# A new order of operations for a fused Nyström attention and MLP kernel on one core

## The chip, the core and the metric

The kernel runs on one core of a Trainium2 chip. A core has a matrix engine (PE, with its weight loads shown as PEld), three engines for elementwise work (DVE, ACT and POOL), and SyncE (SP), which here only issues DMAs. Each engine has its own queue of instructions and works through it in program order; engines wait for one another through semaphores. The metric is the device time of one execution, in microseconds (us), as the median of several runs.

## What is computed

Eight batches of eight heads, 576 rows and 64 columns a head, first through a Nyström attention with 32 landmarks, then through an MLP with a layer norm before and the input added behind. Cut to what matters:

```python
q_lm = q.reshape(B, H, 32, 18, 64).mean(axis=3)
k_lm = k.reshape(B, H, 32, 18, 64).mean(axis=3)
A, Bm, C = sm(q, k_lm), sm(q_lm, k_lm), sm(q_lm, k)      # softmax of the scaled products
Z = Bm.T / (norm1(Bm) * norm_inf(Bm) + 1e-06)
for _ in range(6):
    Z = 2 * Z - Z @ Bm @ Z
attn = A @ Z @ C @ v
x = attn.transpose(0, 2, 1, 3).reshape(B, S, 512)
xn = (x - mean(x)) / sqrt(var(x) + 1e-06) * g_ln
out = x + relu(xn @ w_ch1) @ w_ch2                       # 512 -> 2048 -> 512
```

## The kernel before

**Tiling.** Batch 0 is worked by itself, then batch 1, then the sets of batches 2-3, 4-5 and 6-7 (the text calls these sets 2, 3 and 4, and batch 1 is a set of its own). For each set the attention part makes landmarks (lm, or tot and lmt in batch 1), the landmark products (psb, then the Gram matrix and six steps of the iteration), the weights C (psec, whose exponentials are ec, turned into ecT), their product with v (pscv), the last two small products (pszt and pszc, giving zt and zcbd) and the weights A (psea, whose exponentials ea are normalized through psd, lns and a multiplication). The iteration is a chain between two engines: PE's *step* writes `it`, DVE or ACT forms the *next* `st` from it, and the next step reads that.

The MLP follows by batch: psy gives x, which DVE measures (BATCH_NORM_STATS2, BATCH_NORM_AGGREGATE); psm, corrected by the less terms, gives m, the landmark part already multiplied by w1; psh = ea times m gives the hidden rows in two halves of 288, which ACT or DVE passes through a relu into hT; pso sums hT against w2 in sixteen pieces, and one DVE operation (the *done* of the block) adds x and writes the output rows, which a DMA stores. Four row blocks of batches 2 to 7 use a scheme of seven products instead (ps7a, ps7c, ps7e, with the sums mix on POOL and DVE). The last row block, 7-4, is done in two column parts, pso_74a (384 wide) and pso_74b (128 wide), and comes last.

**Small tiles.** pso, psh, psy, psd and the seven products use the whole 128 x 128 array. psm uses tiles of 64 x 32; psec, psea, the steps of sets 2 to 4, the Gram products and zc and zt use 32 x 32; pscv uses 64 x 64. On PE a run of such matmuls between whole-array ones is called a block of small tiles.

**Weights.** w1 comes in eight loads (load_w1_0 to load_w1_7, stg slots) on SP's queue, each followed by two scalings by g, scale_w1 at L357, on any of three engines. The less-mean matmuls (psf) read the scaled parts. Two slots of v, six of stg, two PSUM slots of kind p2 (for psh and psec among others) and four PSUM banks are the shared buffers of most interest (L296 to L305).

**What sets the order.** Every operation is defined once by a name, the engines that it may run on, and the buffers it uses. A list, ORDER (L19), names 1571 operations by number, each with a letter for its engine (P, D, A, G for POOL, S for SP). The operations are emitted in exactly this order:

```python
order = [(names[int(x[:-1])], x[-1]) for x in ORDER.split()]
for n, e in order:
    emit(n, e)
```

So the list decides each engine's program order, which engine does an operation that several can do, and which buffer of a pool it gets: `emit` (L174) takes the slot that was given back first, and gives a buffer back when its last user has been emitted. An operation that reuses a slot waits for the last user of its former content. Operations on DVE, ACT and POOL, and the DMA issues that stand in their queues, wait for the operation ahead of them even where their own inputs are ready.

At the start, `warm` (L309) puts idle matmuls (idle<-zeros) on PE at several places of the list.

Of the kernel before, what the change touches and what calls it, by code (L numbers as in the profile page):

```python
# [19 lines left out]
0G 20P 23P 4S 12P 14P 24P 17P 11P 2S 1S 3S 6S 7S 10P 21P 28G 38P 25A 26D 34P 39D 40P 29P 30A 31P 27D  # L20
37P 32P 42D 41D 18P 33D 43P 65P 44A 45D 66A 61P 67P 46P 47P 250G 48D 22P 19P 15P 62A 68A 69A 71D
245G 49P 50D 63P 35P 13P 79G 80D 51P 52D 64A 36A 81P 70D 53P 72P 73A 5S 95S 54D 8P 9D 105A 106G 55P
56D 57P 74P 82D 260P 83D 58D 16P 84D 96S 59P 75A 76A 60D 85P 251D 86D 89P 90D 87P 88D 126P 261A 262D
108G 77G 94S 103G 93S 97S 101G 91D 92D 78D 107A 102G 127P 128P 129P 130A 167P 141P 142A 252P 253A
145P 169D 104A 168D 98S 254D 149P 150D 147P 148A 172P 173A 176P 247P 177A 248A 259D 255D 174P 175A
246D 256P 257A 146A 170P 171D 109G 110G 121P 122P 123P 111G 124P 268P 156P 258D 151D 249D 267P 112A
125A 275A 269A 270A 271A 157D 277A 158D 131P 132P 133P 134P 178P 163P 278D 279D 117G 273A 433G 274A
99S 113G 135A 180D 263S 164A 159P 280P 281D 160A 165P 166A 114G 264A 100S 115G 116G 265S 118G 136P
137P 266G 161P 179D 429G 119G 138P 139P 162D 282P 283D 140A 181P 182A 183P 284P 276D 285A 143P 187P
184D 286P 144A 188A 272D 152D 185P 186A 287D 297P 298D 299D 189P 191D 190D 288P 289A 294P 290P 295A  # L30
201P 202P 296A 300P 301A 291D 292P 293A 120G 455G 212P 213P 435G 436G 437G 310P 438G 445G 302A 303G
308P 309A 214P 330P 434D 444D 312D 311D 313D 332D 192P 193A 153D 154D 198P 199A 155A 441D 430D 439D
431D 331D 442D 440D 432D 443D 234P 556D 215P 304P 235P 236P 305A 306A 196P 446G 447G 203P 204P 194P
195A 237P 238P 205P 206P 451G 197A 307G 314P 315A 337P 339P 448G 449D 822G 338A 555D 239P 240P 241P
322P 207P 208P 574D 565D 569G 450D 340A 323A 216P 242D 209D 210S 217P 324D 341P 343D 223P 335P 244S
336A 342D 333P 463D 218P 219P 577G 452D 220D 344P 352P 353D 467G 468G 469G 470G 334A 826G 348P 345A
349A 346P 347A 457G 318P 319A 224P 316P 317A 225P 226P 227P 481P 458G 465D 459G 460G 482A 350P 454D
354D 357P 471D 464D 472D 351A 453D 363P 228P 229P 364D 358A 361P 230P 362A 461D 462D 365D 493P 494A
359P 368P 360A 483P 495P 355P 325D 326D 505A 369A 356A 231D 233A 200G 374P 375P 366P 367A 370P 371A
573G 506D 456D 507P 508P 509D 320P 321D 385P 484P 486A 487A 489A 510P 834D 511D 466D 491A 386P 387P  # L40
485A 388P 211S 512P 376P 473S 474G 490A 377P 496P 498A 501A 499A 497A 513D 514P 327D 488D 492D 328D
396P 397P 475S 476G 566G 828G 829G 830G 831G 572G 477S 478G 838G 839G 844G 564G 568G 503A 378P 379P
380P 515D 823D 502A 221S 504D 372P 516P 479S 480A 500D 517D 836D 528P 529P 530D 531D 398P 399P 373A
381P 522P 518P 389P 329A 866S 382D 418P 519D 824D 559D 520P 521D 523A 532P 419P 420P 524A 533A 534A
558D 550P 551D 552D 553D 548P 549A 421P 422P 423P 536P 424P 425P 848G 535G 832D 833D 554D 232S 867A
537A 538A 539G 560D 525P 527A 400P 401P 557D 426D 427S 605P 526A 606A 840G 841G 594P 595A 561D 540P
541A 390P 391P 611P 612A 837D 596D 827D 392P 393D 825D 850G 851G 852G 563D 603P 604A 853G 562D 859D
842D 860G 861G 843D 579P 613P 614A 407P 580A 601P 602A 609P 610A 1217G 585P 408P 845D 599P 409P 607P
600A 410P 411P 586A 597P 608A 542A 543G 856D 615P 598A 576G 626P 616A 412P 413P 581P 627A 402P 862G
394S 582A 570G 567D 617D 589D 835D 863G 858D 590D 618P 619A 634P 635A 643P 583P 584A 620P 621A 624P  # L50
414P 571G 874P 625A 622P 623A 628P 629A 644P 544P 847D 857D 545A 846D 591D 546A 875D 403P 632P 872S
633A 645P 630P 647P 592D 631A 646P 415D 877P 648P 649P 650P 864D 865D 854D 404D 855D 1191G 886P 638D
637G 641G 663P 664P 665P 639D 640D 662G 428S 417S 406S 661D 593A 882A 884A 879A 880A 883A 652D 878A
651D 657D 887A 889P 892A 896A 658D 666P 668D 894A 895A 849D 667D 653P 654P 711P 722P 712A 723A 891A
890A 655P 656P 547G 575G 675P 676P 677P 728P 729A 678P 695P 696A 1192D 713D 716P 881D 1194D 717A
724P 725A 876P 888P 1213G 660D 587P 870S 714P 416S 659D 871G 873G 384S 1229G 642G 1230G 1231G 726P
898A 715A 679D 682D 669P 897D 727A 588A 730P 222S 1232G 899D 900P 901P 731A 718P 732P 902D 743P 719D
578G 903P 904D 670P 720P 734A 733A 721D 744A 671P 672P 673D 699P 700A 893D 739P 636G 1203D 1239S
701P 905P 243S 741P 906D 740A 751P 674D 742A 703P 752A 907P 735P 736A 737P 383S 868S 681S 680S 683S
738A 702D 908D 909P 1219G 1195G 1220G 1221G 685P 704D 697P 698A 915P 917A 916A 910D 911P 1222G 759P  # L60
760P 749P 811P 925P 750A 761P 885D 869G 921P 926A 927A 753G 922P 1225D 755G 912D 913P 705D 706D 745P
746A 1227D 812P 707D 708D 709D 710A 813P 814P 747P 748A 686P 687P 688P 928G 929P 930A 1223D 1224D
1196D 1233D 815P 816P 923D 1228D 924D 914D 931A 1214D 943P 947D 944D 941P 817P 946D 945D 1240G 754G
756G 932G 758G 942A 762P 692D 767D 694S 689D 818P 763P 764P 918P 765P 766P 395S 1241S 1197G 920A
1198G 1199G 1200G 919A 819D 963P 974P 965A 975A 1207G 1208G 1209G 768D 769P 964D 774D 770P 956P 968P
1215D 1204D 957A 966P 690S 693S 405S 773D 969A 1226D 779P 967A 933P 934A 935A 780P 972P 948P 949A
1234D 1216D 970P 781P 973A 936G 984P 985A 820S 771P 971D 757D 986D 980P 772P 978P 782P 954P 776D
1242A 775D 981A 979A 976P 977A 955A 937P 1193D 938A 939A 1205D 785P 786P 787P 788P 982P 983A 1255P
989P 990A 1210G 684S 783D 1211D 1212D 1201D 1202D 1243P 777G 778G 784D 790D 691S 991P 1244A 789D
992A 801P 1235S 995P 996A 1245P 940G 1236G 1256D 1257P 802P 1267A 1268D 987P 988A 803P 993P 994A  # L70
1066P 1067D 804P 808D 1269P 1270P 1237S 1238G 1246P 1249A 805D 791P 792P 810S 1206D 1271D 821S 1248A
1247A 1253A 1250D 1251A 793P 958D 794P 1006G 1252A 809S 1003P 1004A 1272P 798D 1273D 997P 998A 950P
951A 1001P 1218D 795D 1012P 999P 1002A 1000A 1007G 1009G 1274P 1008D 1275D 952P 953A 1072P 1258P
1073A 1265A 1264A 1276P 1013P 1014P 1015P 1263A 1261A 1260A 1064P 959D 960D 1016P 1259A 961D 962A
1017P 1284P 1285A 1065A 1277D 1278P 1018P 1019P 797S 800S 799S 1294P 1295A 1296A 1021D 1262D 1020D
1026D 1027D 1254D 1279D 1266D 1011G 1022P 1297G 1070P 1023P 1024P 1025P 1029D 1028D 1005G 1068P
1069D 1286A 1298P 1290P 1299A 1291P 1292D 1010D 1293D 1280P 1281D 1091P 1032P 1033P 1038P 1300A
1301G 1092A 1287P 1071D 1289A 1288A 1282P 1283D 1039P 1040P 1312P 1314D 1313D 1316D 1315D 1080P
1082A 796S 1099P 1100A 1081A 1034P 1035P 806S 1310P 1311A 1097P 1036D 1098A 1041P 1306P 1101P 1307A
1095P 1096A 1037D 1030D 1044P 1043D 1093P 1094A 1089P 1090A 1042D 1074D 1075D 1031G 807S 1045P 1046P  # L80
1083P 1084D 1047P 1103A 1051D 1317P 1318A 1087P 1088A 1102D 1085P 1086A 1054P 1052S 1055P 1106P
1107A 1104P 1048D 1049S 1105D 1319P 1320A 1056P 1057P 1061D 1076D 1108P 1058D 1109A 1110P 1111A
# [1181 lines left out]
```

## Time and profile before

| | us |
|---|---|
| median of 3 runs | 259.85 |
| lowest and highest | 259.77 and 260.1 |
| the profiled execution | 260.21 |
| its span in the profile | 258.5 |
| last matmul of block 7-4 ends | 254.6 |

The profiled execution is one more run, 0.36 us above the median. Its span, counted from the first instruction to the last, leaves 1.7 us around it. In the views of the profile a line such as L193 is that of the helper which records every matmul, so rows are told apart by tile names: `pso<-w,hT` writes the tile pso from w and hT. "x4" at a row's end is a run of like instructions, shown as one row with the time from the first one's start to the last one's end. A bracket tells how long the engine had been idle before the row, and what released it. Matmuls are pipelined, so the duration of one overlaps the next; distances between starts tell more.

### The profile page before, as it was taken

To read this page: it belongs to the slowest core of one execution; us is meant where nothing else is said; L and a number is where in the kernel's file an instruction comes from. 1 tells how busy PE (TensorE), PEld (TensorE's weight loads), DVE (VectorE), ACT (ScalarE), POOL (GpSimd) and SP (SyncE) were. 2 spreads that over 40 slices of the span, in tenths; PEclk is the share of its full clock that TensorE was granted. 3 is DMA by queue.
4 is the path that set the end of the run, shared out by engine and by line. 5 is a ranking of instruction groups with operands and counts; after the bars stand their busy time and mean duration, and the time that the engine had idled before them with its cause. 6 is when DMAs were issued, how large, how long until landed. Compare 5 with 4: busy or idle time off the path is not lost.

```text
span 258.5 us, 8352 instructions
## 1 busy us (share of the span) xinstructions
PE 249.3 (96%) x3499; PEld 178.4 (69%) x3499; DVE 212.1 (82%) x472; ACT 164.0 (63%) x304; POOL 177.6 (69%) x180
## 2 busy tenths in 40 slices
PE   7689999999999999999999999999999999999994
PEld 7566565555654457777776787777867787788882
DVE  1669899999999989996998879887537999878761
ACT  1588886737766899778756996878766246544000
POOL 8324899689893789699999996782068505966600
PEclk9999999999999999999999999999999999999998
DMA  6999999999749275949814832400130100500356
GB/s 236 364 281 341 365 207 202 207 230 258 230 121 161 44 160 80 207 100 279 144 21 111 235 96 63 114 16 3 41 85 0 44 20 3 122 22 14 90 120 185
DMA packets 23278, 36.32 MB, mean 140 GB/s; under 512 B 2117, under 2 KB 11593, under 8 KB 23241
## 3 DMA queue, kind: packets, MB, share of 16 engines
q1 hardware_dynamic: 12376, 23.34, 29.9%
q0 software_dynamic: 9504, 10.36, 25.3%
q10 hardware_dynamic: 1360, 2.10, 3.2%
q8 instruction: 27, 0.44, 0.7%
q14 instruction: 11, 0.08, 0.1%
HBM read 36.70 MB, written 9.44 MB: 178 GB/s over the span
## 4 chain that ended last, share of the span: by engine, by line
PE 88%; DMA 6%; ACT 2%; DVE 1%; issue 0%; POOL 0%; ACTq 0%; POOLq 0%
PE psh L193 24%; PE ps7a L193 16%; PE pso L193 15%; PE ps7c L193 8%; DMA nat_q<-in_q_dram 5%; PE ps7e L193 4%; PE psm L193 4%; PE psy L193 3%; PE it L193 3%; PE psec L193 2%; PE pscv L193 2%; DMA stg_k<-in_k_dram 2%; PE psd L193 1%; PE psea L193 1%; PE psf L193 1%; PE pso_74a L193 1%
## 5 line engine op out<-in xcount | busy, mean ns | idle before, releaser
L203 ACT ACTIVATE hT<-psh 128x576 f16<-128x576 f32 x106 | 65.8, 650 | 30.4 <-PE psh L193 28.6
L193 PEld LDWEIGHTS <-hT 128*128 128x128 f16 x688 | 64.4, 98 | 23.3 <-issue 3.7
L193 PE MATMUL psh<-ea,m 128*128 128x288 f16 x512 | 78.3, 287 | 0.1
L193 PEld LDWEIGHTS <-m 128*128 128x128 f16 x512 | 48.8, 98 | 15.7 <-issue 1.3
L193 PE MATMUL pso<-w,hT 128*128 128x512 f16 x176 | 45.7, 380 | 0.1
L207 POOL TENSOR_TENSOR mix<-hT 128x1024 f16<-128x1024 f16 x8 | 17.0, 2128 | 27.4 <-ACT hT L203 27.4
L210 DVE SCALAR_TENSOR_TENSOR x<-ps7a,rstd,x 128x256 f32<-128x256 f32 x48 | 21.3, 476 | 6.2 <-PE ps7a L193 4.4
L193 PE MATMUL ps7a<-mix,hT 128*128 128x256 f16 x192 | 25.6, 273 | 0.0
L1068 DVE TENSOR_SCALAR hT<-psh 128x576 f16<-128x576 f32 x22 | 16.4, 753 | 10.1 <-PE psh L193 9.9
L997 DVE BATCH_NORM_STATS2 six<-x 128x6 f32<-128x512 f32 x36 | 24.2, 673 | 0.0
L207 POOL TENSOR_TENSOR ea<-ea,lns 128x576 f16<-128x576 f16 (+1 forms) x14 | 17.7, 1261 | 8.0 <-ACT lns L203 4.3
L200 ACT CAST m<-psm 128x512 f16<-128x512 f32 (+1 forms) x25 | 19.1, 792 | 4.5 <-PE psm L193 3.4
L200 ACT COPY x<-psy 128x512 f32<-128x512 f32 (+1 forms) x29 | 16.8, 587 | 7.7 <-PE psy L193 7.3
L193 PEld LDWEIGHTS <-mix 128*128 128x128 f16 x192 | 18.3, 98 | 4.3 <-issue 1.5
L207 POOL TENSOR_TENSOR mix<-mix,hT 128x1024 f16<-128x1024 f16 x8 | 17.0, 2127 | 6.2 <-DVE mix L207 5.8
L207 POOL TENSOR_TENSOR hT<-hT 128x1024 f16<-128x1024 f16 x9 | 19.1, 2123 | 0.2
L207 POOL TENSOR_TENSOR hT<-hT,mix 128x1024 f16<-128x1024 f16 x7 | 15.1, 2169 | 4.4 <-PE ps7e L193 2.5
L214 DVE TENSOR_REDUCE part<-xT_k 128x32 f16<-128x576 f16 x24 | 17.1, 736 | 0.0
L207 POOL TENSOR_TENSOR asum_q<-asum_q 128x256 f32<-128x256 f32 (+1 forms) x24 | 15.1, 629 | 1.5
L203 ACT ACTIVATE ec<-psec 128x256 f16<-128x256 f32 (+1 forms) x42 | 12.4, 431 | 5.3 <-PE psec L193 5.3
L193 PE MATMUL psy<-zcbd,ea 128*128 128x256 f16 x80 | 14.8, 273 | 0.2 <-ACT x L200 0.2
L357 POOL TENSOR_SCALAR w<-w1s,g_sb 128x512 f16<-128x512 f32 x12 | 8.2, 693 | 9.4 <-DMA w1s<-in_moe_w_ch_dram 5.5
(174 smaller groups left out, 473.1 us busy)
## 6 DMA issues: line engine op xcount, KB each, us to landing
out_dram<-x SPq DMA_DIRECT2D x55, 128.0 KB, 2.6
stg_v<-in_v_dram SPq DMA_DIRECT2D x10, 576.0 KB, 5.9
w1s<-in_moe_w_ch_dram SPq DMA_DIRECT2D x8, 512.0 KB, 11.6
nat_q<-in_q_dram POOLq DMA_DIRECT2D x7, 576.0 KB, 8.3
nat_k<-in_k_dram POOLq DMA_DIRECT2D x7, 576.0 KB, 8.2
w<-in_moe_w_ch_dram POOLq DMA_DIRECT2D x4, 512.0 KB, 9.0
out_dram<-x ACTq DMA_DIRECT2D x15, 128.0 KB, 2.4
stg_v<-in_v_dram SPq DMA_DIRECT2D x6, 288.0 KB, 4.3
```

The costliest lines, as they stand in the source:

```text
L193: keep(nc.tensor.matmul(o, l, r, start=start, stop=stop, tile_position=(rb, cb), skip_group_check=(skip or cb != 0)))
L200: keep(nc.scalar.copy(o, i) if e == "A" else ENGINES[e].tensor_copy(out=o, in_=i))
L203: keep(nc.scalar.activation(*args, **kw))
L207: keep(ENGINES[e].tensor_tensor(out=o, in0=a, in1=b, op=f))
L210: keep(ENGINES[e].scalar_tensor_tensor(out=o, in0=a, scalar=s, in1=b, op0=f0, op1=f1))
L214: keep(nc.vector.tensor_reduce(out=o, in_=i, axis=axis, op=f))
L357: keep(ENGINES[e].tensor_scalar(out=o, in0=src, scalar1=g_sb[:, kk:kk + 1], scalar2=0.0, op0=ALU.mult, op1=ALU.add))
L997: keep(nc.vector.bn_stats(out=T(f"six_{j}")[:], in_=T(f"x_{j}")[:]))
L1068: keep(nc.vector.tensor_scalar(out=o, in0=T(psh)[:, :, 0:HS], scalar1=0.0, scalar2=None, op0=ALU.max))
```

## The change

Nothing but the list ORDER differs. The 1571 operations are the same; the first and the last lines of the list show how it is written:

```diff
 ORDER = """
-0G 20P 23P 4S 12P 14P 24P 17P 11P 2S 1S 3S 6S 7S 10P 21P 28G 38P 25A 26D 34P 39D 40P 29P 30A 31P 27D
...
+4S 0G 23P 14P 17P 2S 26A 11P 28G 20P 24P 12P 1S 25D 3S 7S 10P 16P 15P 6S 38P 39A 21P 40P 34P 5S 42A
...
 """
```

Nearly every entry has another place. 136 operations have another engine: among them 18 relu go from DVE to ACT and 15 from ACT to DVE, 8 and 4 copies of x likewise, 15 casts of m change sides, 13 mixing sums of the seven products go from POOL to DVE and 11 back, 3 norms and some scalings of w1 change, and 17 stores that SP issued are issued by ACT, 8 the other way. In operations, PE has 622 before and after, DVE 398 and 387, ACT 312 and 332, POOL 153 and 153, SP 86 and 77. The idle matmuls that stood between batch 0's steps stand earlier. SP issues all eight loads of w1 ahead of batch 1's two loads of v, where one of the v loads stood between the seventh and the eighth; the w1 loads themselves come as 2, 3, 0, 1, 7, 4, 5, 6 instead of 2, 3, 1, 0, 4, 5, 6, 7.

Three places show what that is like. The first is ACT's queue at the start of batch 1, at about 20 to 30 us (w_16_78 is the scaled w1, tot the landmark sums of batch 1, x and hT belong to batch 0, less is the correction of m). Before:

```order
L200 CAST tot_q<-psl_q 128x128
L203 ACTIVATE w_16_78<-w1s,g_sb 128x512
L200 COPY x<-psy 128x512
L203 ACTIVATE hT<-psh 128x576 x2
L200 CAST tot_k<-psl_k 128x128
L203 ACTIVATE hT<-psh 128x576
L200 CAST tot_k<-psl_k 128x128
L200 COPY x<-psy 128x512
L203 ACTIVATE w_16_78<-w1s,g_sb 128x512
L200 CAST less<-psf 128x512
L203 ACTIVATE ec<-psec 128x2x2x32
```

and now:

```order
L203 ACTIVATE w_16_78<-w1s,g_sb 128x512
L200 CAST tot_q<-psl_q 128x128
L203 ACTIVATE hT<-psh 128x576
L200 COPY x<-psy 128x512
L203 ACTIVATE hT<-psh 128x576
L200 CAST less<-psf 128x512
L200 CAST tot_k<-psl_k 128x128
L203 ACTIVATE hT<-psh 128x576
L200 CAST tot_k<-psl_k 128x128
L203 ACTIVATE w_16_78<-w1s,g_sb 128x512
L203 ACTIVATE ec<-psec 128x4x2x32
```

The first scaling shown is now of load 1, the fourth in SP's queue, and stands ahead of the second tot_q; the second is of load 5, the seventh in the queue, and stands directly ahead of the ec, where the less stood between.

The second place is PE in set 2, the second step of the iteration (`it<-st`, 32 x 64). Before, it stood by itself behind three pairs of pso:

```order
L193 LDWEIGHTS hT_1334
L193 MATMUL pso_1649<-w2_16_79,hT_1334 128x512
L193 LDWEIGHTS st_1709
L193 MATMUL it_1543<-st_1709 32x64
L193 LDWEIGHTS st_1709
```

and now it follows the second psec directly, which itself follows the first step:

```order
L193 LDWEIGHTS lm_1560
L193 MATMUL psec_1751<-xT_k_1476,lm_1560 32x288
L193 LDWEIGHTS st_1743
L193 MATMUL it_1579<-st_1743 32x64
L193 LDWEIGHTS st_1743
```

One step, psec and one step thus make one block of small tiles, where there had been two with whole-array matmuls between.

The third place is DVE behind set 2's zc, at about 82 us (zcbd comes from zc; `w<-w,less` is the centering of w1 with the less terms, done once for all later batches; `x<-pso` is a done; m comes from the psm of batch 2). Before:

```order
L207 TENSOR_TENSOR zcbd<-pszc,heads_71 128x256 x3
L220 STREAM_TRANSPOSE sT_q<-s_q 128x64
L214 TENSOR_REDUCE part<-sT_q 128x64
L207 TENSOR_TENSOR zcbd<-pszc,heads_71 128x256
L207 TENSOR_TENSOR w_16_78<-w_16_78,less 128x2x512 x2
L210 SCALAR_TENSOR_TENSOR x<-pso,rstd,x 128x512
L207 TENSOR_TENSOR w_16_78<-w_16_78,less 128x2x512
L220 STREAM_TRANSPOSE xT_q<-nat_q 128x576
L200 CAST m<-psm 128x512
```

and now:

```order
L210 SCALAR_TENSOR_TENSOR st<-st,it 128x4x32
L220 STREAM_TRANSPOSE xT_q<-nat_q 128x576
L207 TENSOR_TENSOR zcbd<-pszc,heads_71 128x256 x4
L207 TENSOR_TENSOR w_16_78<-w_16_78,less 128x2x512
L210 SCALAR_TENSOR_TENSOR x<-pso,rstd,x 128x512 x2
L200 CAST m<-psm 128x512
```

All four zcbd and one centering now stand ahead of the done, and other work of this stretch has gone elsewhere in the queue.

More of the change, by code (lines that the diff above doesn't have):

```diff
@@ L25 @@
[L25 to L34, printed above, removed]
@@ new lines @@
+1207G 967A 1208G 954P 1209G 1210G 681A 986A 1216D 970P 1202D 971D 955A 972P 936G 786P 1211D 1212D
+950P 233S 973A 951A 777G 787P 993P 994A 1204D 778G 937P 1255P 938A 783D 939A 940G 788P 784D 1243P
+1244A 987P 988A 791P 789D 989P 790D 793P 1256D 952P 953A 1257P 990D 1245P 1267A 1235S 958D 995P 996A
+991P 801P 794P 1268D 992A 1228D 802P 1246P 1247A 1252A 1253A 1270P 1251A 1269P 961D 1271D 792P 798D
+795D 1248A 1249A 803P 804P 999P 1003P 1238G 1000A 805D 1272P 1066P 1254D 960D 1004A 1067A 1006G
+1001P 808D 810S 1273D 1002A 997P 998A 1064P 1012P 1072P 1010G 1008G 1274P 1065A 1007G 1250D 1073A
@@ new lines @@
+1312P 1314D 1310P 1311A 1080P 1082A 1005G 1046P 1313D 1315D 1316D 1095P 1044P 1045P 797A 1096D 1306P
+1047P 1097P 1048D 1050S 1081A 1051D 1307A 1098A 1087P 1011G 1039P 1088D 1089P 1090A 1101P 1103D
+1083P 1084A 1085P 1086A 1319P 1317P 1041P 1102D 1108P 1109A 1043D 1320D 1318A 1110P 1180P 1181P
+1308A 1111D 1104P 1105A 1042D 1106P 1054P 1107A 1056P 1078D 1112P 1113A 1075D 1343P 1344D 1122D
+1332P 1057P 1124D 1182P 1120P 1053A 1121A 1116P 1117A 1055P 1061D 1062A 1309G 1183P 1058D 1118P
+1184P 1119A 1114P 1076D 1115A 1334D 1132P 1134P 1074D 1302P 1333A 1128P 1049A 1123D 1125D 1303A
@@ new lines @@
+1304A 1339P 1340D 1328D 1185P 1186P 1187P 1337P 1079A 1188D 1338A 1190S 1130P 1345P 1131P 1059S
+1129P 1136D 1346A 1127G 1321P 1341P 1133P 1137D 1342D 1146G 1140P 1335P 1135P 1143D 1351P 1141P
+1322A 1142D 1336D 1353P 1138P 1139P 1352A 1145D 1189S 1347P 1348A 1148P 1150P 1305G 1144D 1151P
+1354D 1325P 1355A 1356P 1357D 1349P 1149P 1350A 1329D 1126G 1156P 1364P 1157P 1154P 1155P 1365A
+1366P 1367A 1153D 1147G 1433P 1434A 1327D 1152D 1360P 1162P 1361D 1358P 1359D 1326D 1163P 1372P
+1373A 1158D 1060S 1160P 1370P 1371A 1159D 1161P 1362P 1167D 1169S 1323P 1363A 1324D 1368P 1164D
@@ new lines @@
+1165S 1369D 1170P 1168A 1460P 1461D 1449P 1375G 1451A 1381P 1172P 1171P 1450A 1435P 1376G 1173P
+1174D 1379G 1452P 1453A 1454P 1385P 1330D 1436D 1455A 1456P 1052A 1457D 1382P 1063S 1464P 1465A
+1437P 1377G 1468P 1444D 1383P 1458P 1387P 1469A 1177D 1331A 1384P 1390D 1389D 1438A 1459A 1466P
+1386P 1467D 1443D 1470P 1471A 1481P 1388P 1462P 1179A 1401P 1396D 1403P 1472A 1404P 1393P 1402P
+1391P 1395D 1178A 1441P 1442A 1378G 1482D 1392P 1479P 1463D 1405D 1175S 1480A 1166S 1176A 1394P
+1473P 1474A 1406D 1447D 1398D 1475P 1399G 1476A 1439P 1415P 1477P 1478A 1374G 1485P 1486A 1497P
@@ new lines @@
+1498P 1400D 1487P 1488A 1397D 1409P 1380D 1410P 1407P 1408P 1411D 1440A 1446D 1413P 1414P 1412D
+1445D 1448A 1499P 1416P 1420D 1489P 1422S 1500P 1505D 1483P 1425P 1417D 1491G 1495D 1517P 1493G
+1418S 1423P 1424P 1484A 1519P 1506D 1509P 1507P 1490A 1501P 1492D 1494D 1426P 1510P 1419S 1427D
+1430D 1431A 1421A 1502P 1508P 1432A 1496G 1503P 1504P 1520P 1513D 1515G 1514D 1518P 1511D 1523P
+1524P 1429S 1521D 1522D 1428S 1525P 1526P 1516D 1527D 1531P 1532P 1528D 1529P 1530P 1512D 1533D
+1534A 1536D 1537G 1549P 1539P 1540P 1541P 1542P 1543D 1546D 1550P 1551P 1552P 1553P 1554P 1555P
@@ L105 @@
+1556P 1557D 1548A 1538S 1560P 1535S 1561P 1544A 1558A 1545S 1562P 1563P 1564P 1565P 1566P 1547G
+1559S 1567P 1568D 1570S 1569A
 """
```

126 lines of the change are left out of this document (52 added, 74 removed).

## The prediction

> **What bounds the kernel now.** The page first (busy times, ACT's busy tenths and the granted clock, in 40 slices of 6.46 us), then the windows: length; then busy us and instructions of PE, weight loads, DVE, ACT and POOL; then clock, DMA share, GB/s.
>
> ```profile
> PE 249.3 (96%) x3499; PEld 178.4 (69%) x3499; DVE 212.1 (82%) x472; ACT 164.0 (63%) x304; POOL 177.6 (69%) x180
> ...
> ACT  1588886737766899778756996878766246544000
> ...
> PEclk9999999999999999999999999999999999999998
> ```
>
> ```profile
> 0.00:42.00 42.00, 36.88 (x650) 26.05 (x651) 30.50 (x84) 28.59 (x53) 26.73 (x56) 1.00 1.06 291
> ...
> 54.00:90.00 36.00, 35.88 (x599) 19.84 (x592) 34.55 (x73) 24.89 (x49) 28.60 (x33) 1.00 0.77 174
> 90.00:130.00 40.00, 40.00 (x562) 28.69 (x563) 36.18 (x78) 33.18 (x64) 35.91 (x36) 1.00 0.76 159
> 130.00:180.00 50.00, 49.90 (x945) 37.52 (x934) 42.77 (x105) 38.59 (x73) 41.00 (x29) 1.00 0.32 84
> 180.00:251.00 71.00, 71.00 (x661) 57.51 (x659) 54.31 (x108) 31.85 (x54) 36.36 (x18) 1.00 0.20 48
> 251.00:258.50 7.50, 3.63 (x34) 2.42 (x31) 1.84 (x4) 0.00 (x0) 0.00 (x0) 0.90 0.67 192
> ```
>
> From 54 us to 251 us PE is busy but for 0.22 us. The new list keeps PE's 622 operations and every matmul in them, and the tail is the same, so only three things can move the end: what PE loses within its busy time, waits that come or go, and the startup, the only stretch where PE stands idle by microseconds (5.12 of 42). An engine made lighter elsewhere brings nothing.
>
> What is lost within busy time is seen in PE's timeline, as the distance from one start to the next (durations overlap, and "x4" is a run of like instructions).
>
> ```profile
> 53.35 0.60 PE L193 MATMUL pso<-w,hT 128*128 128x512 f16 x2
> 53.88 0.41 PE L193 MATMUL psm<-w,zt 64*32 64x512 f16 x8
> 54.22 0.61 PE L193 MATMUL pso<-w,hT 128*128 128x512 f16 x2
> ...
> 69.11 0.70 PE L193 MATMUL psec<-xT_k,lm 32*32 32x288 f16 x32
> 69.64 0.28 PE L193 MATMUL it<-st 32*32 32x64 f16 x16
> 69.85 1.47 PE L193 MATMUL pso<-w,hT 128*128 128x512 f16 x6
> ...
> 71.25 0.30 PE L193 MATMUL it<-st 32*32 32x64 f16 x16
> 71.48 1.04 PE L193 MATMUL pso<-w,hT 128*128 128x512 f16 x4
> 72.44 0.70 PE L193 MATMUL psec<-xT_k,lm 32*32 32x288 f16 x32
> ...
> 93.72 1.03 PE L193 MATMUL pso<-w,hT 128*128 128x512 f16 x4
> 94.58 0.65 PE L193 MATMUL psh<-ea,m 128*128 128x288 f16 x4
> 95.16 0.63 PE L193 MATMUL psm<-w,zt 64*32 64x512 f16 x16
> 95.72 1.04 PE L193 MATMUL pso<-w,hT 128*128 128x512 f16 x4
> ...
> 104.98 0.70 PE L193 MATMUL psec<-xT_k,lm 32*32 32x288 f16 x32
> 105.62 1.48 PE L193 MATMUL ps7e<-w,hT 128*128 128x256 f16 x12
> ...
> 119.02 0.72 PE L193 MATMUL psm<-w,zt 64*32 64x512 f16 x16
> 119.67 0.29 PE L193 MATMUL it<-st 32*32 32x64 f16 x16
> ```
>
> Four pso take 0.86 us (93.72 to 94.58), so a pair takes 0.43; the pair at 53.35 takes 0.53. Going from 128-row matmuls to small tiles therefore costs 0.10. One psm takes 0.34 from its start to the next pso (0.44 with the way in); two together take 0.56 (0.66), where two apart would take 0.88: **one block of small tiles fewer saves 0.22**. A step (it<-st) alone takes 0.23 + 0.10 = 0.33. A psec alone takes 0.64 + 0.10 = 0.74, and with a step behind it 0.53 + 0.21 + 0.10 = 0.84, again 0.23 under the sum. A step behind a psm pair saves less: the pair, which took 0.56 with the way out, takes 0.65 to the step's start (119.02 to 119.67), and the step still follows; 64-row and 32-row tiles are changed between at a price of their own.
>
> **The change part by part.**
>
> *Blocks of small tiles.* Counting them in PE's new order from 54 us on, there are 41 where there were 45. Set 2: its Gram matrix joins psec and a step joins the second psec, while one step is left alone: one block fewer, -0.22. Set 3: two fewer, of which one joins the psm pair (0, as at 119.67) and one joins the products, -0.22. Set 4: a step joins psec (-0.23) and zt stands beside zc and psm (about -0.13, since those tiles differ), -0.36. Batch 6's psm pair is split: +0.22. Ahead of 54 us batch 1's zc, zt and first psm become one block: -0.2. **Sum -0.78**, bounds -1.1 (every merge at 0.22 or more) and -0.4 (changed kinds save nothing).
>
> The Trainium skill, "TensorEngine Tiling (Array Packing)", section "Tiling Modes", says that changing the tiling mode, but not the tile, drains TensorE. The 0.65 at 119.02 agrees. By that rule read strictly, zt beside zc saves its full 0.22, and the sum would be some 0.1 lower.
>
> *Waits that go.* PE's one clear wait in this stretch is between these two rows:
>
> ```profile
> 83.80 1.32 PE L193 MATMUL pso<-w,hT 128*128 128x512 f16 x4
> 85.04 0.50 PE L193 MATMUL psea<-xT_q,lm 32*32 32x288 f16 x32
> ```
>
> Four pso and the way in are 0.96, and 1.24 passed: 0.28. Other work now stands ahead of it, so I count **-0.25**; at worst 0.
>
> *Waits that come.* Set 2's second psec has fewer pso behind it than before.
>
> ```profile
> 76.16 1.25 PE L193 MATMUL pscv<-natv,ecT 64*64 64x130 f16 x72
> ```
>
> ```profile
> 73.19 1.72 ACT L203 ACTIVATE ec<-psec 128x256 f16<-128x256 f32 x6 [1.61 <-PE psec L193]
> 74.69 1.22 ACT L200 CAST natv<-stg_v 128x1152 f16<-128x1152 f32 x1
> ```
>
> From psec's start (72.44) ACT needs until 75.91, 3.47 us, for the six ec and the cast of v that the second half of the products (pscv) reads. PE reached that half about 0.6 after 76.16, 4.3 us behind psec. In the new order there stand between them psec and a step (0.64), three pso pairs (1.29), psh (0.49), a step with its way in and out (0.31) and half the products (0.55): 3.28. So PE waits **0.2**; if DVE, which turns the ec between, is late as well, 0.4. The psh on ACT behind the cast waits with it.
>
> ```profile
> 82.13 1.09 DVE L207 TENSOR_TENSOR zcbd<-pszc,heads 128x256 f16<-128x256 f32 x3
> ...
> 85.15 0.75 DVE L210 SCALAR_TENSOR_TENSOR x<-pso,rstd,x 128x512 f32<-128x512 f32 x1
> 85.82 1.52 DVE L207 TENSOR_TENSOR w<-w,less 128x1024 f16<-128x1024 f16 x1
> ```
>
> Set 2's psm needs the PSUM bank that block 1-4's last sum (x<-pso at 85.15) frees. In the new order DVE takes four zcbd, one centering (w<-w,less) and then that sum: 4 x 0.36 + 0.70 + 0.70 = 2.8 with the centering at its usual length, 3.7 with the 1.52 it took at 85.82. PE offers 3.36 between zc and psm. So the wait is 0 or some 0.4; I take 0.15. Steps that stand close behind one another wait for DVE's next:
>
> ```profile
> 17.92 0.24 PE L193 MATMUL it<-st 32*32 32x64 f16 x8 [0.40 <-DVE st L210]
> ```
>
> There PE stood 0.40 for a round trip with a smaller tile; two new pairs of steps with only a psec (0.53) between come short by about 0.1 each. **Sum of new waits 0.55**, bounds 0.1 and 1.2.
>
> *The startup.* Loads, their sizes and the first 18 us of queues are nearly alike, so what lands when is read from the rows of before. The order of the eight w1 loads changes from 2,3,1,0,4,5,6,7 to 2,3,0,1,7,4,5,6, all ahead of batch 1's v.
>
> ```profile
> 25.15 2.71 POOL L357 TENSOR_SCALAR w<-w1s,g_sb 128x512 f16<-128x512 f32 x4 [1.41 <-DMA w1s<-in_moe_w_ch_dram]
> ```
>
> ```profile
> 24.42 1.19 ACT L203 ACTIVATE hT<-psh 128x576 f16<-128x576 f32 x2
> ...
> 27.95 0.72 ACT L203 ACTIVATE w<-w1s,g_sb 128x512 f16<-128x512 f32 x1 [0.75 <-DMA w1s<-in_moe_w_ch_dram]
> ...
> 31.68 1.19 ACT L203 ACTIVATE hT<-psh 128x576 f16<-128x576 f32 x2 [0.33 <-PE psh L193]
> ```
>
> The fourth load lands at 25.1, the sixth at 27.9 (both waits end there), so the seventh at about 29.3. ACT now scales a part of w1 from the fourth ahead of its first hT, which so starts at 25.9 instead of 24.42; PE's cover is the psh and the less-means that stand there anyway. And it scales part 5, now in the seventh load, ahead of all six ec: 29.3 + 0.6 + 1.7 for the ec, a softmax row and a less (0.5) puts its next hT at 32.2, where it was 31.68. PE's path carries about 0.5 of that. Back come the round trips of the first iteration, whose steps DVE now answers one after another, up to 0.7 in all, and ACT's gaps behind 31.68. Following the rows in the new order, batch 1's first psm starts about when it did, at 42.5, with one pso pair (0.43) less done ahead of it. **+0.4**; bounds -0.5 (round trips saved, ACT's lateness hidden) and +1.5 (the first hT's 1.5 in full).
>
> *Engines.* Of 136 moved operations the balance is some 7 us less on DVE and 8 more on ACT. Only where ACT is full can this cost; that is a rival.
>
> **Sum** against the profiled execution: -0.78 - 0.25 + 0.55 + 0.4 = -0.08 us on 260.21. That execution is 0.36 above the median of the runs, so the forecast is 259.85 - 0.1 = **259.75 us**.
>
> **The rivals.**
>
> 1. *The startup is not later and the chains hold*: -0.78 - 0.25 + 0.1 - 0.1 = -1.0, 258.8 us. For it: DVE, 34.55 of 36 us busy in 54 to 90, is the engine that is relieved. Against it: no slack was found at the places named.
> 2. *ACT's waits for w1 reach PE in full* (slower): the startup's +1.5 instead of +0.4, 260.85, and with the new waits at their upper end 261.5. It decides from the point where the psh ahead of the late hT fill both PSUM slots, at about 26 us. Against it: PE has the less-means to do there.
> 3. *ACT becomes the bound*: its digits are 9 and 9 at 142 to 155 us, and it gets some 3 us more work between 140 and 165. It would show as waits of psh and psy for ACT; a third of that would be +1.0, 260.75. Against it: followed operation by operation, PE's path keeps its distance from ACT there but for 0.1.
> 4. *The clock falls in the startup*. The idle matmuls before 20 us are nearly all gone from their old places, and PE is thinly used at 19 to 23 us.
>
> ```profile
> 1.40 3.82 PE L193 MATMUL idle<-zeros 128*128 128x128 f16 x38 [1.40 <-DVE zeros L252]
> ```
>
> These 38 ran at 0.10 us each, so about half as fast as the clock later allows; such a stretch again would cost some 1.9 us, 261.6. The profile's clock is 1.00 in all windows to 251, through 5 us of idle PE. The Trainium skill, "TensorE: Matmul & The Clock Gate", Part 1, says that an idle window of about 3.4 us throttles to half; by that rule this comes only if a gap that long opens, and the trace has none near it.
> 5. *The change does little of what it says*: few places. It does not hold; nearly the whole list reads differently, but the terms above come to nothing.
>
> **How the numbers follow.** A measurement of this kernel tells 0.2%, 0.52 us, from no change: faster is under 259.33, slower over 260.37. The forecast's case (terms as summed, within about 0.5) has 0.42; the first rival 0.32; the second 0.14, the third 0.07, the fourth 0.05. Of the forecast's case a few hundredths lie beyond either bound, so faster 0.35, same 0.39, slower 0.26. The range of 8 in 10 takes in the first rival and most of the second: 258.6 to 261.1. The likeliest case alone is 259.3 to 260.3.
>
> **What would show it.** Right: PE's busy share still whole from 54 us, 41 blocks, batch 1's first psm near 42.5, waits of 0.1 to 0.4 at the second psec of set 2 and its psm. Wrong: a psh waiting for ACT's hT at 26 to 32 us by over 1 us; a clock digit under 9; waits of PE over 0.5 us behind 54 us; or batch 1's first psm well ahead of 42 us.

## The result

| | before | changed |
|---|---|---|
| median of 10 runs, us | 259.84 | 261.99 |
| lowest and highest, us | 259.64 and 261.6 | 261.53 and 262.66 |
| profiled execution, us | 260.21 | 261.9 |
| its span, us | 258.5 | 260.2 |

The changed kernel is **slower**: 1.0066 of before, 95% interval 1.0046 to 1.0087. The forecast was no change (259.75 us, range 258.6 to 261.1).

The page of the changed kernel has these lines in place of those shown of before (busy us, granted clock):

```profile
PE 250.3 (96%) x3499; PEld 179.4 (69%) x3499; DVE 210.4 (81%) x461; ACT 168.5 (65%) x317; POOL 173.5 (67%) x180
...
PEclk9997999999999999999999999999999999999999
```

And its windows (length; busy us and instructions of PE, PEld, DVE, ACT, POOL; clock, DMA share, GB/s):

```profile
0.00:42.00 42.00, 37.67 (x641) 26.75 (x642) 28.73 (x79) 29.51 (x56) 27.09 (x56) 0.96 1.03 288
42.00:54.00 12.00, 11.42 (x97) 6.52 (x81) 10.70 (x21) 9.06 (x17) 8.98 (x12) 1.00 1.22 216
54.00:90.00 36.00, 35.97 (x592) 18.96 (x591) 32.85 (x72) 23.18 (x47) 27.58 (x32) 1.00 0.80 170
90.00:130.00 40.00, 38.85 (x530) 28.35 (x529) 38.13 (x77) 34.48 (x68) 29.19 (x32) 1.00 0.69 146
130.00:180.00 50.00, 49.97 (x955) 37.83 (x953) 43.15 (x102) 38.67 (x75) 44.85 (x32) 1.00 0.34 93
180.00:251.00 71.00, 71.00 (x661) 56.98 (x660) 54.15 (x107) 33.58 (x59) 34.64 (x18) 1.00 0.22 51
```

Before, the window that the prediction leaves out read:

```profile
42.00:54.00 12.00, 12.00 (x82) 6.41 (x81) 11.91 (x26) 6.88 (x14) 9.03 (x12) 1.00 1.22 205
```

Two stretches stand out. In 90 to 130 us, where PE never waited before, it is now idle for 1.15 us. In 42 to 54 us it is idle for 0.58 us, where it had none. The clock dips to 0.7 in the fourth slice. Elsewhere the picture is that of before, and DVE is a little lighter and ACT heavier, as counted.

The last matmul ends 1.8 us later in the profile. Where this came from is read at two moments, batch 1's second psm and the last matmuls. PE's timeline of the changed kernel, then of before:

```profile
54.98 0.47 PE L193 MATMUL psm<-w,zt 64*32 64x512 f16 x8
...
255.38 1.06 PE L193 MATMUL pso_74b<-w,hT 128*128 128x128 f16 x16
```

```profile
41.90 0.60 PE L193 MATMUL pso<-w,hT 128*128 128x512 f16 x2
42.47 0.41 PE L193 MATMUL psm<-w,zt 64*32 64x512 f16 x8
...
253.57 1.06 PE L193 MATMUL pso_74b<-w,hT 128*128 128x128 f16 x16
```

The second psm stood at 53.88 before, 1.10 us earlier; PE has by now done two psh more and two pso pairs less, 0.12 us of work, so **the startup, up to here, lost 0.98 us** between these two profiles. (Two kernels below that keep the order of before up to here, e9 and e10, have this psm at 54.20 and 54.12, so some 0.3 us of it is a difference between executions.) The last matmul ends at 256.44 instead of 254.63, 1.81 later. Behind 55 us the loss is thus 0.71, and 0.83 at equal work. The one wait in 90 to 130 us is 1.15 us of idle time in it. In e7 below, where that wait is gone, the way from the second psm to the start of pso_74b is 199.02 us instead of 200.40, so **the wait costs 1.38 us in all, and everything else behind 55 us gained 0.55**. The three parts, 0.98, 1.38 and -0.55, make up the 1.81.

The wait, in the views of PE, DVE and POOL (start, us, engine, line, operation, tiles; in brackets the idle time ahead of it and its releaser):

```profile
119.33 0.22 PE L193 MATMUL it<-st,bones 128*128 128x128 f16 x1 [1.07 <-DVE st L207]
```

```profile
114.06 0.86 DVE L210 SCALAR_TENSOR_TENSOR x<-ps7a,rstd,x 128x256 f32<-128x256 f32 x2
114.84 3.70 DVE L200 CAST natv<-stg_v 128x1152 f16<-128x1152 f32 x1
118.46 0.28 DVE L214 TENSOR_REDUCE rsum<-it 128x4 f32<-128x128 f32 x1
...
118.99 0.29 DVE L207 TENSOR_TENSOR st<-it,rcr 128x128 f16<-128x128 f32 x1
```

```profile
114.69 0.74 POOL L207 TENSOR_TENSOR asum_q<-asum_q 128x256 f32<-128x256 f32 x1
115.35 1.05 POOL L200 COPY hT<-hT 128x1024 f16<-128x1024 f16 x1
116.35 0.46 POOL L207 TENSOR_TENSOR asum_q<-asum_q 128x128 f32<-128x128 f32 x1
116.76 1.15 POOL L207 TENSOR_TENSOR mix<-w,mix 128x512 f16<-128x512 f16 x1
117.87 0.94 POOL L207 TENSOR_TENSOR s_q<-asum_q,nat_q 128x128 f16<-128x128 f32 x1
```

PE's Gram matrix of set 3 needs DVE's softmax (rsum, its reciprocal rcr, st), which stands behind a cast of v that took 3.70 us. The only cast of v that DVE did before, at 15.2 us, took 0.76. This is one of the operations that changed engines (the two lists differ in 137 of them, one more than the text above says): cast_v41, which POOL did at 126.6 us in 1.16. Before, on DVE and on POOL:

```profile
15.16 0.76 DVE L200 CAST natv<-stg_v 128x1152 f16<-128x1152 f32 x1
```

```profile
126.58 1.16 POOL L200 CAST natv<-stg_v 128x1152 f16<-128x1152 f32 x1
```

While the cast of the changed kernel is drawn out, POOL runs operation after operation, each starting 0.04 to 0.08 us before the one ahead has ended; only behind the fourth does the cast end, and the fifth is itself drawn out, 0.94 where this sum takes 0.42 to 0.43.

At the end of the startup, PE and SP in the changed kernel, then SP before:

```profile
42.49 0.41 PE L193 MATMUL psm<-w,zt 64*32 64x512 f16 x8
42.84 0.66 PE L193 MATMUL psh<-ea,m 128*128 128x288 f16 x4
43.87 0.59 PE L193 MATMUL pso<-w,hT 128*128 128x512 f16 x2 [0.37 <-DMA w<-in_moe_w_ch_dram]
```

```profile
36.60 0.37 SPq L223 DMA_DIRECT2D stg_v<-in_v_dram  x1
```

```profile
55.84 2.94 SPq L223 DMA_DIRECT2D stg_v<-in_v_dram  x4
```

Batch 1's first psm starts at 42.49 (42.47 before), as forecast, with a pso pair less behind PE. But that pso then waits for the second part of w2, which before had landed by 41.90. The trace has its time from issue to landing as 8.3 us before (from 33.5) and 11.2 now (from 32.7). And SP sends a load of 576 KB, batch 2's first v, at 36.60: before it stood behind three stores and went out at 55.8, as the first of the four shown.

### The profile page after: what moved, and what is told of

It reads as the page before. It is cut to its first block, busy times and chain, and to the rows that moved or that the text cites. A ratio compares the mean times of both kernels' runs of the same rounds, so it can differ in the third digit from the quotient of the medians.

```text
span 260.2 us, 8347 instructions
## 1 busy us (share of the span) xinstructions
PE 250.3 (96%) x3499; PEld 179.4 (69%) x3499; DVE 210.4 (81%) x461; ACT 168.5 (65%) x317; POOL 173.5 (67%) x180
## 4 chain that ended last, share of the span: by engine, by line
PE 78%; DMA 11%; DVE 3%; issue 3%; POOL 3%; POOLq 0%
PE psh L193 21%; PE ps7a L193 16%; PE pso L193 14%; PE ps7c L193 8%; DMA w1s<-in_moe_w_ch_dram 5%; DMA w<-in_moe_w_ch_dram 4%; PE ps7e L193 4%; PE psy L193 3%; PE psm L193 3%; PE it L193 2%; DMA stg_k<-in_k_dram 2%; DVE natv L200 1%; PE pscv L193 1%; POOL w L357 1%; PE psd L193 1%
## 5 line engine op out<-in xcount | busy, mean ns | idle before, releaser
L203 ACT ACTIVATE hT<-psh 128x576 f16<-128x576 f32 x109 | 68.3, 656 | 31.3 <-PE psh L193 30.7
L207 POOL TENSOR_TENSOR ea<-ea,lns 128x576 f16<-128x576 f16 (+1 forms) x17 | 20.2, 1190 | 16.0 <-ACT lns L203 16.0
L207 POOL TENSOR_TENSOR hT<-hT 128x1024 f16<-128x1024 f16 x9 | 20.2, 2247 | 13.2 <-DVE mix L207 13.0
L207 POOL TENSOR_TENSOR mix<-hT 128x1024 f16<-128x1024 f16 x7 | 14.8, 2127 | 16.0 <-ACT hT L203 16.0
L200 ACT COPY x<-psy 128x512 f32<-128x512 f32 (+1 forms) x33 | 19.4, 587 | 7.4 <-PE psy L193 7.3
L207 POOL TENSOR_TENSOR hT<-hT,mix 128x1024 f16<-128x1024 f16 x9 | 19.1, 2129 | 3.5 <-DVE mix L207 2.8
L200 ACT CAST m<-psm 128x512 f16<-128x512 f32 (+1 forms) x26 | 18.1, 729 | 4.2 <-PE psm L193 4.1
L200 POOL CAST natv<-stg_v 128x1152 f16<-128x1152 f32 (+1 forms) x11 | 12.7, 1167 | 7.4 <-DMA stg_v<-in_v_dram 7.2
L1068 DVE TENSOR_SCALAR hT<-psh 128x576 f16<-128x576 f32 x19 | 14.3, 754 | 2.9 <-PE psh L193 2.5
L207 POOL TENSOR_TENSOR asum_q<-nat_q 128x512 f32<-128x512 f16 x12 | 13.9, 1157 | 3.1 <-DMA nat_q<-in_q_dram 3.0
```

The costliest lines, as they stand in the source:

```text
L200: keep(nc.scalar.copy(o, i) if e == "A" else ENGINES[e].tensor_copy(out=o, in_=i))
L203: keep(nc.scalar.activation(*args, **kw))
L207: keep(ENGINES[e].tensor_tensor(out=o, in0=a, in1=b, op=f))
L1068: keep(nc.vector.tensor_scalar(out=o, in0=T(psh)[:, :, 0:HS], scalar1=0.0, scalar2=None, op0=ALU.max))
```

## The experiments

Each kernel was timed beside the kernel before on the same chip, so the ratios are compared; the changed kernel's is 1.0066. In the diffs, entries of the list are shown by name with their engine, with a few neighbours of those that moved.

**The stretched cast.** The first theory (A) is that it held up DVE and with it PE, and (A1) that POOL's work stretched it. Two experiments on the changed kernel: e1 gives the cast to POOL, e2 leaves it on DVE and adds a small copy on POOL that reads the cast's output, so that POOL's queue has to wait.

```diff
 add7_220 D
-cast_v41 D
 ...
 norm_31_0 G
+cast_v41 G
```

> The changed kernel with one operation moved: set 3's cast of v (natv<-stg_v at 114.84 us, 3.70 us on DVE) goes to POOL, behind the norm that ends at 112.3, where POOL is idle for 1.5 us. Theory A (the stretched cast held up DVE, and PE's Gram matrix waited 1.07 us for DVE's softmax): that wait goes, the cast takes about 1.2 us on POOL, and the time falls by 0.9 to 1.2 us, to about 260.9. Rival B (the wait was due to the whole order of DVE there, and DVE would have been late anyway): the wait stays at 0.5 us or more and the time falls by under 0.4.

```diff
+    op("hold", "G", (), lambda e: copy(e, hold_t[:], natv_buf[0][:, 1, 0, 0, 0:D]))
 ...
+hold G
 asum_q711 G
```

> The changed kernel with the cast of v left on DVE and one small copy added on POOL, which reads what the cast writes and so holds POOL's queue (five elementwise operations in a row from 114.69 us) until the cast is done. Theory A1 (the cast is stretched because POOL works at the same time): the cast takes 0.75 to 0.8 us instead of 3.70, PE's wait of 1.07 us at the Gram matrix goes, and the time falls by 0.8 to 1.2 us. Rival A2 (the cast is slow for a reason of its own, such as its transfer or the place of its data): it still takes over 3 us, POOL is late as well, and the time stays or rises.

e1 came to 1.0043 (1.0026 to 1.0059), e2 to 1.0034 (1.0020 to 1.0048): 0.6 and 0.8 us less than the changed kernel. The intervals overlap with the changed kernel's (1.0046 to 1.0087), so the times alone would not settle it. The profiles do: in both, PE's wait is gone altogether, and the way from the second psm to the start of pso_74b is 199.04 and 199.03 us, 1.36 and 1.37 under the changed kernel's. The window 90 to 130 us of e1, and DVE and POOL in e2:

```profile
90.00:130.00 40.00, 40.00 (x537) 29.12 (x536) 36.08 (x78) 35.74 (x70) 31.57 (x33) 1.00 0.70 158
```

```profile
115.68 0.75 DVE L200 CAST natv<-stg_v 128x1152 f16<-128x1152 f32 x1
```

```profile
116.50 0.23 POOL L200 COPY hold_t<-natv 128x64 f16<-128x64 f16 x1 [0.99 <-DVE natv L200]
```

The same cast on the same engine takes 0.75 us once POOL is silent. A2 falls. e2's time fell as expected, e1's by less than the 0.9 expected at least; its startup took some back (its profile has 0.92 us of waiting for w2, where the changed kernel's has 0.37, and its second psm at 55.62, 0.64 later).

The cross-check gives the cast to DVE in the kernel before, at its old place:

```diff
 ecT_21 D
-cast_v41 G
+cast_v41 D
```

> The kernel before with the same cast of v given to DVE at its place there (126.6 us), while POOL goes on with sums of 2.1 us each. Theory A1 (a cast on DVE and POOL's work hold each other up): the cast takes well over 1 us, up to the end of a POOL operation (2 us or more), or a POOL operation is stretched by 0.7; the time rises by 0 to 1 us, as the next steps of the iteration stand behind it on DVE. Rival A2 (something of the place in the changed kernel alone): it takes 0.76 us and the time stays within 0.2 us.

1.0117 (1.0085 to 1.0149). DVE and POOL:

```profile
128.51 2.66 DVE L200 CAST natv<-stg_v 128x1152 f16<-128x1152 f32 x1
```

```profile
128.42 2.12 POOL L207 TENSOR_TENSOR mix<-hT 128x1024 f16<-128x1024 f16 x1
130.62 2.52 POOL L207 TENSOR_TENSOR mix<-mix,hT 128x1024 f16<-128x1024 f16 x1
```

The cast lasts 0.63 us past the end of POOL's operation at 130.54, and POOL's next is 0.4 longer than its usual 2.12: each keeps the other out. The Trainium skill, "SBUF — State Buffer", section "Who interferes with whom", says that a DVE cast in a two-port mode and a POOL operation share a pair of ports, and that whichever starts first holds it for the whole instruction. These rows agree, and add that in the changed kernel the wait did not end with one POOL instruction but went over four that followed without a gap. The time of e3 rose by 3.0 us, more than forecast (0 to 1). Soon behind the cast PE waits twice there where it had not, 1.24 us for ACT's hT at 137.97 and 0.59 for lns at 139.83, 1.83 together, about what the cast was late. Followed row by row against the kernel before, PE falls back by 2.07 us at these two places and by nothing behind them. The profiled execution, 3.9 us longer than before's, had lost 2.1 already at batch 1's first psm (44.58, clock 0.68 at 20 to 25 us), which has nothing to do with the cast; of the four runs, the two with a mean clock of 0.997 or more took 262.47 and 262.67 us, the other two over 264.1. So some 2 us of the 3 belong to the cast, still more than forecast.

**The startup.** Two kernels change the list at a seam behind batch 1's first psm. e4 takes the order of before up to there and the changed order for the rest; e5 the reverse.

```diff
-order = changed
+order = before[:272] + [op for op in changed if op not in before[:272]]    # e4
+order = changed[:269] + [op for op in before if op not in changed[:269]]   # e5
```

> The order of before up to batch 1's first psm and the operations next to it (272 operations), then all others in the changed order with its engines. Theory S (the changed startup costs 0.8 us: one pso pair of 0.43 not yet done at 42.5 us, then 0.37 of waiting for w2): the time falls by 0.6 to 1.0 us against the changed kernel, to about 261.1, with the stretched cast still there. Rival C (the startup costs more, since PE's clock falls to 0.68 at 20 to 25 us in the profile of the changed kernel): it falls by 1.5 us or more, to 260.4 or less. Rival N (the startup makes no difference at the end): within 0.3 us of 262.0.

> The changed order up to batch 1's first psm and the operations next to it (269 operations), then all others in the order of before, so that batch 2's v stays behind the stores. Theory S (the changed startup costs by itself): 0.4 us more than before for the pso pair not yet done, up to 1 us where k of batch 1 lands late. Theory D (most of the loss at 42 us is the early load of v): within 0.3 to 0.5 us of before, and no wait for w2 at 43 us.

Between them, e6 moves one entry of the kernel before:

```diff
 load_v11 S
+load_v20 S
 store_0_0 S
 ...
-load_v20 S
 cast_v20 G
```

> The kernel before with one entry moved: batch 2's first load of v (576 KB, issued by SP at 55.8 us behind three stores) stands ahead of the first store, as in the changed list, where it went out at 36.6 us. Theory D (that load takes transfer time from the second part of w2, which PE needs at about 42 us): the w2 part lands 1 to 2 us later than 41.8, PE's pso waits 0.4 to 1.0 us for it, and the time rises by 0.3 to 1.0 us. Rival (transfers have room, or the startup's other changes made the wait): no wait of PE for w2, time within 0.2 us of before.

e4 came to 1.0097 (1.0072 to 1.0122), not faster than the changed kernel as expected: theory S, as it stood, fell. Its profile has a wait of 0.98 us for w2, at a startup whose order is that of before, so the cause had to lie in what the rest of the list sends early. e6 says what: 1.0047 (1.0025 to 1.0069) for one load. e5, with the changed startup but the load behind the stores, is 1.0011 (0.9993 to 1.0030), which leaves the changed order of the startup itself with -0.2 to +0.8 us.

The profile of e6 was taken in an execution that was late from the start (first psm at 44.58) and shows no wait for w2. A second profile of the same kernel is e12:

> The kernel of e6 again, for a second profile: e6 was 1.0 us slower than before, but its profiled execution was late from the first 20 us on (clock 0.96, a wait for the scaling of w1). Theory D: with an ordinary start, PE waits for the second part of w2 at 41.9 to 43 us, by 0.4 us or more. Rival D2 (the early load delays something else): no such wait, and PE is late before 40 us or behind 43.

SP and PE there:

```profile
35.32 0.37 SPq L223 DMA_DIRECT2D stg_v<-in_v_dram  x1
```

```profile
42.97 0.59 PE L193 MATMUL pso<-w,hT 128*128 128x512 f16 x2 [0.48 <-DMA w<-in_moe_w_ch_dram]
```

With only that load moved, PE waits 0.48 us for w2 at the place where the kernel before did not (41.90). The landing of w2's second part agrees in every profile: with the startup of before it takes 7.8 to 8.3 us from its issue where the load of v is late (before, e3, e8, e9, e10), and 8.8 to 9.4 where it is early (e4, e6, e12). Together with the next one this carries theory D. In e12 PE stood 0.5 us behind the profile of before already ahead of this wait. So how much of e6's 1.2 us is the wait, and how much is other loads of the startup that also share the transfers, stays open.

e7 makes both repairs in the changed kernel, e8 in e4:

```diff
-load_v20 S
 ...
-cast_v20 A
 ...
 store_3_0 S
+load_v20 S
 load_v21 S
 ...
+cast_v20 G
 load_v30 S
 ...
-cast_v41 D
 ...
 norm_31_0 G
+cast_v41 G
```

> The changed kernel with two repairs: set 3's cast of v on POOL, as in e1, and batch 2's first load of v behind the first store, with its cast on POOL ahead of the next load. Theory D with A: the wait for w2 (0.4 us in the changed kernel's profile, 0.9 in e1's) goes as well, so the time is 0.4 to 0.8 us under e1's, about 1.001 of before. Rival: w2 lands as late as before because of POOL's own order of issues (w2, q, w2, k), and the time is that of e1.

> The startup of before (272 operations), then the changed order with both repairs of e7. If the startup, the early load and the stretched cast are all that cost, what is left are 0.6 us of fewer blocks of small tiles and two waits less against some 0.6 us of new waits of the steps: from 0.6 us under before to equal. Rival (the changed order loses elsewhere too): slower than before by over 0.5 us.

e7 is at 1.0017 (0.9999 to 1.0035), 0.7 us under e1, though the intervals overlap. In its profile the pso at the end of the startup no longer waits, and set 3's Gram matrix starts 1.25 us earlier than at 119.33, behind a ps7a that starts level (117.65 and 117.66):

```profile
43.37 0.66 PE L193 MATMUL psh<-ea,m 128*128 128x288 f16 x4
43.87 0.59 PE L193 MATMUL pso<-w,hT 128*128 128x512 f16 x2
...
118.08 0.22 PE L193 MATMUL it<-st,bones 128*128 128x128 f16 x1
...
254.00 1.06 PE L193 MATMUL pso_74b<-w,hT 128*128 128x128 f16 x16
```

The pso itself starts at 43.87 as in the changed kernel, since this execution came to its first psm 0.53 us later (43.02). So the missing wait alone would prove little; the landing does more: with the changed startup, w2's second part took 9.7 to 10.0 us from its issue where the load of v is late (e5, e7, e11), and 11.2 to 12.0 where it is early (the changed kernel, e1, e2). By the ratios the two repairs take away nearly three quarters of the loss, and what is left cannot be told from no change with certainty. In the profile all of the gain over the changed kernel, 1.38 us at pso_74b, is the cast's; against e1, which is 0.64 later at the second psm, the load's share shows. e8 is at 1.0015 (0.9998 to 1.0033), not under before as hoped: at its seam, at 55 us, PE waited 0.38 us for a PSUM bank that DVE frees, which neither parent has.

**The price of a block and of a joined step.** e10 takes six psm pairs of the kernel before apart; e11 takes e7 and sets three steps one whole-array operation later.

```diff
-psh_600 P
 psm_62 P
+psh_600 P
 psm_63 P
```

> The kernel before with six pairs of psm (batches 2, 3, 6 and 7) taken apart: in each the first psm is set one whole-array operation earlier, so PE has six more blocks of small tiles and nothing else. Theory T (each block costs 0.22 us on a PE that never waits): six times 0.22, 1.3 us more, about 1.005 of before. Rival (the change of tiles is hidden behind the weight loads or by other waits): under 0.5 us more.

```diff
 psec_11 P
-step_2_1 P
 pso_10_10 P
+step_2_1 P
```

> The kernel of e7 with three steps of the iteration (the second of sets 2 and 3, the third of set 4) set one whole-array operation later on PE, away from the psec or psm that they were joined to. Theory W (joining saved 0.22 us of block, and cost 0.2 us of waiting for DVE's next): the time stays within 0.3 us of e7. Rival W1 (the waits are the larger): 0.4 us or more faster. Rival W2 (the steps did not wait there): 0.5 us slower.

e10 came to 1.0125 (1.0109 to 1.0140), 3.2 us and not 1.3. At one of the six places nothing but the blocks changed, and there the price holds; PE in e10, and the same place before:

```profile
206.58 1.47 PE L193 MATMUL ps7a<-mix 128*128 128x256 f16 x12
207.99 0.41 PE L193 MATMUL psm<-w,zt 64*32 64x512 f16 x8
208.33 0.66 PE L193 MATMUL psh<-ea,m 128*128 128x288 f16 x4
208.92 0.41 PE L193 MATMUL psm<-w,zt 64*32 64x512 f16 x8
209.26 1.05 PE L193 MATMUL ps7a<-mix,hT 128*128 128x256 f16 x8
```

```profile
205.47 0.65 PE L193 MATMUL psh<-ea,m 128*128 128x288 f16 x4
206.06 0.62 PE L193 MATMUL psm<-w,zt 64*32 64x512 f16 x16
206.61 0.61 PE L193 MATMUL ps7a<-mix,hT 128*128 128x256 f16 x4
```

Apart, the second psm starts 0.59 behind a psh of 0.49 and takes 0.34, the first the same: 0.88 with both ways in. Together it was 0.10 + 0.55. That is 0.23. At the first of the six places, though, a psm set earlier also waited for ACT's ea and for the done that frees its PSUM bank:

```profile
PE psm L193 <- DVE x L210: 0.7, 1, 0.7
PE psm L193 <- ACT ea L203: 0.3, 1, 0.3
```

Followed row by row, PE falls back by 1.39 us at that place and by 0.29, 0.50, 0.23 and, for the last two together, 0.57 at the others; 0.25 is the execution's startup. So one place shows the price of a block by itself, the other places have short waits on top, and the kernel's time does not show the price.

e11 is at 1.0025 (1.0008 to 1.0042), within 0.3 us of e7's, as theory W has it, but with an interval of some 0.6 us around the difference. The profiles say more: at the three steps themselves e11 is level with e7 to 0.06 us, and at set 2's products it loses 0.74. In set 2, in the changed kernel and then in e11:

```profile
73.39 0.69 PE L193 MATMUL psec<-xT_k,lm 32*32 32x288 f16 x32
74.10 0.29 PE L193 MATMUL it<-st 32*32 32x64 f16 x16
```

```profile
73.53 0.69 PE L193 MATMUL psec<-xT_k,lm 32*32 32x288 f16 x32
74.15 0.61 PE L193 MATMUL pso<-w,hT 128*128 128x512 f16 x2
74.68 0.29 PE L193 MATMUL it<-st 32*32 32x64 f16 x16
...
77.87 0.33 PE L193 MATMUL pscv<-natv,ecT 64*64 64x130 f16 x9 [0.50 <-ACT natv L200]
```

psec with a step behind it took 0.53 to the step's start before; here it takes 0.71, so the joined step stands 0.18 for DVE, which eats what the block saved. In e11 it no longer does, and the products then wait 0.50 for the cast of v on ACT, the wait that the prediction saw coming for the changed kernel and that did not appear there. So joining these steps gained nothing in itself, as W says, and in set 2 it hid a wait that shows when they are taken apart.

**The later part alone.** e9 keeps the order of before for 655 operations, to about 103 us.

```diff
-order = changed
+order = before[:655] + [op for op in changed if op not in before[:655]]
 ...
-cast_v41 D
 ...
 norm_31_0 G
+cast_v41 G
```

> The order of before for 655 operations, to about 103 us, then the changed order for the rest, with set 3's cast of v on POOL. Theory: with startup, early load and stretched cast all gone, the later part of the changed list is better by itself, by 0.6 us of fewer blocks against 0.3 of waits of steps: 0.2 to 0.5 us faster than before. Rival (the later part loses too, or the seam does): equal or slower.

1.0031 (1.0016 to 1.0047): the rival. PE waited 0.7 us at the seam for a sum on DVE. No version here beats the kernel before: the changed list gains 0.55 us behind 55 us once the cast is repaired, but here it always came with the changed startup or with a seam, and these cost as much or more.

## Why the prediction was wrong

**What bounds the kernel: right.** PE is busy from 55 us to 251 us but for the cast's wait and 0.06 us besides, and the lighter DVE brought nothing.

**Blocks, waits that go, waits that come: right in kind, and better than forecast.** The forecast for what lies behind 54 us was -0.58 for blocks (the -0.2 of batch 1 lies ahead of it), -0.25 and +0.55, -0.28 in all. Measured without the stretched cast (e7 against before): -0.55. The 41 blocks are there. Two joined steps waited for DVE by some 0.2 each, not 0.1 (74.10 in set 2). The waits at set 2's products and at its psm, 0.2 and 0.15, did not come. The first was over-counted: the prediction takes psec with a step as 0.64 where its own rows give 0.74, and with the step's own wait PE came to the second half of the products some 3.6 us behind psec, when ACT, 3.46 behind, was done. The wait that was to go (0.28) went: PE is idle for 0.03 us in 54 to 90.

**Startup: the mechanism was missed and the size was too small.** The forecast was +0.4, less the 0.2 of the joined block, and it was +0.98 in the profiles, of which the missing pso pair (0.43) and the wait for w2 (0.37) are seen and 0.18 is not traced. The pair was foreseen. The moment of the first psm was hit at 42.49, in part by luck: in the other profiles with this startup order (e1, e2, e5, e7, e11) it is 42.59 to 43.44, and in four of them PE waits 0.7 to 1.1 us for batch 1's k at 27 to 28 us. The step that failed is "Loads, their sizes and the first 18 us of queues are nearly alike, so what lands when is read from the rows of before". It followed the order of w1's loads, and of the queue behind them only those of batch 1. The next entry of SP's queue, batch 2's v, had moved past three stores and so from 55.8 to 36.6 us, into the transfer of w2. e6 and e12 show the cost on the kernel before, and the landing of w2's second part, 0.5 to 2.3 us longer with the early load, shows the way.

**Engines: the step that failed most.** The prediction says "Only where ACT is full can this cost". It counted moved operations at their usual length on the new engine and looked at one engine's fill alone. The cast's 0.76 on DVE came from 15.2 us, where POOL did nothing; at 114.8 us POOL is in a row of operations, and it took 3.70. e1 and e2 take away the resulting wait (1.15 us of idle PE, 1.38 us in all), and e2 shows that POOL's concurrent work is the cause. The row that warned of it was quoted: a centering of 1.52 us where 0.70 is usual, which was used for one term only. Beside it POOL multiplied ea from 85.50 to 86.78; the centering ended 0.56 us behind that.

**Rivals.** The second (ACT's waits for w1) and the third (ACT as the bound) did not come as described: PE's waits for ACT are 0.67 us at 17.95, for a scaling of w1 but ahead of the place that the rival named, and 0.20 at 42.27. The fourth did happen, and costs little: the profile's clock is 0.96 in 0 to 42 us and 0.50 from 22 to 25, but the changed kernel's seven runs with a mean clock of 0.997 or more average 261.9 us and the three at 0.993 262.2, where 1.9 had been priced. The gap of some 3.4 us that the prediction made its condition was not there: PE's longest wait in the ten microseconds ahead of the dip is 0.67.

## What to carry to other kernels

When a list moves an operation to another engine, its length there is to be taken from a place where its neighbours are as busy as at the new one: DVE and POOL stretched each other here, a cast from 0.75 to 3.70 us. In a queue of DMAs an entry that moves past a store or a load counts, also one for a buffer needed much later: the early v stood in the way of a part of w2, which in e12 took 9.4 us to land instead of 8.3. A saving of 0.2 us a piece on a saturated engine is real, but one stretched operation ahead of a softmax undid six of them.

## What was not expected of the hardware

A cast of 0.75 us on DVE took 3.70 us beside five POOL operations that followed one another closely, and 2.66 us beside POOL operations of 2.1 us: it lasted over four of the short ones, and over one of the long ones, behind which POOL had a gap of 0.08 us (130.54 to 130.62). Both times it ended 0.63 us behind the end of the POOL operation that it outlasted last. What lets DVE in is not shown: a gap in POOL's queue would fit the second case, but in the first POOL's fifth operation started 0.04 us before the fourth had ended, and was then itself drawn out.
